# Attention scores per head: one matmul over an interleaved q transpose, or two over 64 partitions each

## The chip, the cores and the metric

The kernel runs as one program on one core of a Trainium2 chip. The metric is the device time of one execution in microseconds (us). A profiled execution has its own time and its own span, the stretch from its first to its last instruction in the trace. Engines are named as in the profile: PE is the matrix engine (PEld its weight loads), DVE the vector engine, ACT the scalar engine, POOL the general engine, SP the engine whose queue issues most DMA transfers.

## The reference, cut to what matters

Three layers run one after the other: local attention, a dense layer with a rational activation, and a gated sum over eight experts. Only the attention is touched.

```python
batch, n_heads, seq, head_dim = (4, 8, 576, 64)
scores = scale * np.matmul(q, k.transpose(0, 1, 3, 2))
rel = pos[:, None] - pos[None, :]
mask_plain = (rel >= 0) & (rel < 32)                      # heads 0 to 3
mask_dil = (rel >= 0) & (rel < 128) & (rel % 4 == 0)      # heads 4 to 7
scores = np.where(mask, scores, -1e9)
attn = softmax(scores)
x = attn @ v          # (2304, 512) after the heads are put side by side
h = x @ w_in;  g = P(h) / Q(h);  y = g @ w_out
out = sum over e of gate[:, e] * (relu(y @ w1[e]) @ w2[e])
```

## The kernel before, in words

**Three stages.** The attention of batch 0 runs first, in the order that `att_pieces(0)` lists. Then come 96 steps of the dense layer (`rat_l1`, `rat_a`, `rat_b`, `rat_c`, `rat_l2`), and the attention of batches 1, 2 and 3 is spread over the slots between them: `ATT` gives batch 1 to steps 0 to 7, batch 2 to steps 7 to 23 and batch 3 to steps 40 to 62. Last come the experts (`moe_l1`, `moe_l2`), in which no attention is left.

**One pair of heads.** Heads are taken in pairs, 16 pairs in all (4 batches of 4). The 64 dimensions of the two heads lie one above the other on 128 partitions. `att_prep` transposes q and k of a pair on PE, half a sequence at a time: three or four transposes (L352) into one PSUM bank, then copies into SBUF. k's transpose `kT` is copied as it is, by ACT (L362). q's transpose `qT` is kept in a blown-up form of shape 128 x 576 x 2: column (s, 0) holds head 0 of position s on partitions 0 to 63 and zeros below, column (s, 1) zeros above and head 1 on partitions 64 to 127. So q's bank is copied twice, the upper half by ACT (L366), the lower half by DVE (L364), each with a stride of two elements; the zeros are set once per tile at the start (L329), since there are two such tiles in all, one for even and one for odd pairs of batches 0 and 1.

**One group of scores.** `att_qk` handles 192 positions of a pair: three blocks of 64 positions, whose scores against 96 keys lie side by side in one PSUM bank, 128 rows (position, head) by 288 columns. First a 16-bit matmul with the identity adds the mask (L374, 128 rows by 288 columns). Then one matmul in 32-bit floats per block (L380) takes 128 columns of the blown-up `qT` as weights and 96 columns of `kT` as the moving operand. The trace shows each such matmul as two weight loads and two passes, so a group has six. There are 48 groups. The softmax follows on DVE (L398), ACT (L400), DVE (L404, L405) and POOL (L406). `att_tr` transposes the probabilities (L415, copied by ACT at L420), and `att_av` multiplies by v with six matmuls of 96 rows by 64 columns (L439, twelve passes), three for each half of the columns of PE; its moving operand is read with a stride of two.

**Order.** PE, DVE, ACT and POOL each work in the order in which they are given instructions. The pieces are laid into slots by hand, and the order of instructions is then fixed by a planner that simulates a timeline (`schedule_with_timeline_sim=True`). SP issues the loads in its own order; loads made by `load()` (L159) also wait for the latest mask matmul of batch 0 or the first matmul of a step (`gate_mm`, L376 and `rat_l1`).

Of the kernel before, what the change touches and what calls it, by code (L numbers as in the profile page):

```python
# [28 lines left out]
def kernel(  # L29
# [14 lines left out]
    nc = tc.nc  # L44
    B, H, S, D = q.shape
# [4 lines left out]
    P = 128  # L50
# [8 lines left out]
    KW = 96  # L59
# [173 lines left out]
    ident = cpool.tile([P, P], F32, name="ident")  # L233
    make_identity(nc, ident)
    nc.vector.memset(one, 1.0)
    ident_b = cpool.tile([P, P], BF16, name="ident_b")
    nc.vector.tensor_copy(ident_b, ident)
    SEAMS = (0, None, None, None, 32, None, 0, None, 16, 48, -16, None)
    masks = cpool.tile([P, 12, KW], BF16, name="masks")
    nc.gpsimd.memset(masks[:, 0], 0.0)  # L240
    nc.gpsimd.affine_select(out=masks[:, 0], in_=masks[:, 0], pattern=[[2, KW]], compare_op=ALU.is_ge, fill=NEG, base=-1, channel_multiplier=-1)
    nc.gpsimd.affine_select(out=masks[:, 0], in_=masks[:, 0], pattern=[[-2, KW]], compare_op=ALU.is_ge, fill=NEG, base=64, channel_multiplier=1)
    nc.vector.tensor_copy(masks[:, 1:12], masks[:, 0:1].to_broadcast([P, 11, KW]))
    for i, x in enumerate(SEAMS):
        if x is None:
            continue
        m = masks[:, i, 0:32 + x]
        if x <= 0:
            nc.gpsimd.memset(m, NEG)
        else:  # L250
            nc.gpsimd.affine_select(out=m, in_=m, pattern=[[0, 32 + x]], compare_op=ALU.is_ge, fill=NEG, base=2 * x - 1, channel_multiplier=-1)
    MASK_AT = {(0, 0): 0, (0, 1): 1, (0, 2): 1, (1, 0): 6, (1, 1): 3, (1, 2): 9}

    abt = cpool.tile([P, 8], F32, name="abt")
# [66 lines left out]

    def att_qk_tiles(alt):
        if alt:
            t = room("W3", [P, 3 * S + 32], F32)
            qT, kT = t[:, 0:2 * S].rearrange("p (s h) -> p s h", h=2), t[:, 2 * S:]
        else:
            qT = room("aqT", [P, S, 2], F32)
            kT = room("akT", [P, S + 32], F32)
        nc.vector.memset(qT, 0.0)  # L329
        nc.vector.memset(kT[:, 0:32], 0.0)  # L330
        return qT, kT

    def att_prep(b, pr, x):
        st = att[b, pr]
        which, y = divmod(x, 2)
        key = "ak" if which else "aq"
        src = st[key]
# [5 lines left out]
        if which == 0:  # L343
            outs = tuple((h * D, (h + 1) * D, st["qT"][:, :, h]) for h in range(2))
        else:
            outs = ((0, P, st["kT"][:, 32:]),)
        if y == 1:
            st.pop(key)
        w, n = (QB, 3) if pr < 2 else (72, 4)
        bt = bank("qkps")  # L350
        for c in range(n):
            nc.tensor.transpose(bt[:, c * w:(c + 1) * w], src[:, n * y + c, :, :].rearrange("p h d -> p (h d)"), ident[:w, :w])  # L352

        def after():
            for p0, p1, d in outs:
                if pr < 2:
                    dv, ps = d[p0:p1, y * HS:(y + 1) * HS], bt[p0:p1, 0:HS]
                else:
                    dv = d[p0:p1, :].rearrange("m (c w) -> m c w", c=4)[:, :, y * 72:(y + 1) * 72]
                    ps = bt[p0:p1, 0:HS].rearrange("m (c p) -> m c p", c=4)  # L360
                if which:
                    nc.scalar.activation(dv, ps, AF.Copy)  # L362
                elif p0 == D:
                    nc.vector.tensor_scalar(out=dv, in0=ps, scalar1=QSCALE, scalar2=None, op0=ALU.mult)  # L364
                else:
                    nc.scalar.activation(dv, ps, AF.Copy, scale=QSCALE)  # L366

        return after

    def att_qk(b, pr, jj):  # L370
# [6 lines left out]
        qf = st["qT"].rearrange("p s h -> p (s h)")  # L377
        for i in range(3):
            j = 3 * jj + i
            nc.tensor.matmul(  # L380
                bt[:, i * KW:(i + 1) * KW],
                qf[:, j * P:(j + 1) * P],
                st["kT"][:, j * 64:j * 64 + KW],
                start=False,
                stop=i == 2,
            )
        sc = bt[:, 0:3 * KW].rearrange("q (i c) -> q i c", i=3)
        i = b * NG + pr * 3 + jj
        sx = sb.tile([P, 4, 3], F32, tag="asx", bufs=4, name="sx")
# [41 lines left out]

    def att_av(b, pr, jj):
        st = att[b, pr]
        pT = st.pop(("pT", jj)).rearrange("k (i q h) -> k i q h", i=3, h=2)
        vt = att.pop(("v", b * NG + pr * 3 + jj))
        bt = bank("avps")
        for h in range(2):
            for i in range(3):
                nc.tensor.matmul(  # L439
                    bt[h * D:(h + 1) * D, i * 64:(i + 1) * 64],  # L440
                    vt[:, i, h, :],
                    pT[:, i, :, h],
                    start=True,
                    stop=True,
                )
# [899 lines left out]
```

## Time and profile before

| | us |
|---|---|
| three runs | 2025.17, 2027.48, 2030.88; median 2027.48 |
| the profiled execution, its own time | 2025.65 |
| its span in the trace | 2023.9 |
| PE busy | 1896.6 (94% of the span) |
| DVE busy | 1625.1 (80%) |
| ACT busy | 1235.8 (61%) |

The shares are averages over stages with different limits, so they have to be read again stage by stage: attention of batch 0 alone until the first step of the dense layer at 66.1 us, steps with the attention of batches 1 and 2 until about 268 us, steps without attention, steps with the attention of batch 3 from about 336 to 478 us, steps without attention, and the experts from 633 us to the end. A row of a window lists the busy time of each engine, the number of instructions in brackets, the granted clock of PE (1.00 is 2.4 GHz, 0.50 is 1.2 GHz), the share of the DMA engines and what they moved. Matmuls are pipelined: the distance from one start to the next says more than the duration of one.

### The profile page before, as it was taken

To read this page: it belongs to the slowest core of one execution; us is meant where nothing else is said; L and a number is where in the kernel's file an instruction comes from. 1 tells how busy PE (TensorE), PEld (TensorE's weight loads), DVE (VectorE), ACT (ScalarE), POOL (GpSimd) and SP (SyncE) were. 2 spreads that over 40 slices of the span, in tenths; PEclk is the share of its full clock that TensorE was granted. 3 is DMA by queue.
4 is the path that set the end of the run, shared out by engine and by line. 5 is a ranking of instruction groups with operands and counts; after the bars stand their busy time and mean duration, and the time that the engine had idled before them with its cause. 6 is when DMAs were issued, how large, how long until landed. Compare 5 with 4: busy or idle time off the path is not lost. (4 is left out here: it accounts for less than half of the span.)

```text
span 2023.9 us, 36375 instructions
## 1 busy us (share of the span) xinstructions
PE 1896.6 (94%) x13914; PEld 1428.6 (71%) x13914; DVE 1625.1 (80%) x2784; ACT 1235.8 (61%) x2328; POOL 486.8 (24%) x490
## 2 busy tenths in 40 slices
PE   7688899998989789999999999999999999999997
PEld 6466667876766566777777777777777777777776
DVE  5898899899998878778877877878778787787754
ACT  5777777776776536565654655556566466565543
POOL 1232233222222003112411511421231241141111
PEclk7688999999999899999999999999999999999999
DMA  6642220124310333146346345435534634543323
GB/s 174 167 142 77 60 75 14 33 65 143 105 41 12 120 105 110 62 127 160 72 109 170 67 104 144 110 62 135 154 64 107 175 78 105 152 87 79 87 55 47
DMA packets 209791, 200.06 MB, mean 99 GB/s; under 512 B 78288, under 2 KB 160208, under 8 KB 209616
## 3 DMA queue, kind: packets, MB, share of 16 engines
q1 hardware_dynamic: 192480, 164.70, 26.9%
q0 software_dynamic: 17136, 33.03, 10.9%
q8 instruction: 109, 1.79, 0.4%
q14 instruction: 66, 0.54, 0.1%
HBM read 151.67 MB, written 46.01 MB: 98 GB/s over the span
## 5 line engine op out<-in xcount | busy, mean ns | idle before, releaser
L925 PEld LDWEIGHTS <-roomA 128*128 128x128 f16 x3276 | 321.9, 99 | 197.6 <-issue 32.2
L925 PE MATMUL l1a<-roomA 128*128 128x384 f16 x1872 | 358.8, 328 | 4.8 <-ACT roomV L974 3.7
L925 PE MATMUL l1b<-roomA 128*128 128x384 f16 x1404 | 277.3, 329 | 14.1 <-DVE roomA L976 6.7
L683 POOL TENSOR_TENSOR roomIG<-roomA,roomIG 128x384 fp32r<-128x384 f32 x96 | 112.2, 1169 | 289.2 <-ACT roomIG L682 214.8
L947 POOL TENSOR_TENSOR roomIG<-roomA 128x384 f32<-128x384 f32 x48 | 60.7, 1264 | 464.4 <-ACT roomA L981 314.1
L1016 PE MATMUL yps<-roomA,roomV 128*128 128x256 f16 x630 | 170.3, 274 | 2.0 <-DVE roomV L1039 1.3
L1016 PE MATMUL yps<-roomA 128*128 128x256 f16 x630 | 169.6, 273 | 2.5 <-DVE roomV L1040 1.5
L1017 PE MATMUL yps<-roomA,roomV 128*128 128x256 f16 x630 | 171.5, 274 | 0.0
L1017 PE MATMUL yps<-roomA 128*128 128x256 f16 x630 | 170.8, 273 | 0.0
L1018 PE MATMUL yps<-roomA,roomV 128*128 128x256 f16 x630 | 170.6, 274 | 0.0
L1018 PE MATMUL yps<-roomA 128*128 128x256 f16 x630 | 169.4, 273 | 1.0 <-DVE roomA L992 1.0
L645 PE MATMUL h1ps<-roomA 128*128 128x384 f16 x384 | 131.5, 343 | 15.4 <-DVE roomA L665 7.9
L698 PE MATMUL o1ps<-roomIG,roomV 128*128 128x384 f32 x384 | 137.1, 357 | 4.3 <-POOL roomIG L683 4.1
L874 POOL TENSOR_TENSOR roomA<-roomA 128x256 f32<-128x256 f32 x140 | 130.1, 948 | 37.3 <-DVE roomA L888 23.6
L646 PE MATMUL h1ps<-roomA 128*128 128x384 f16 x384 | 130.7, 340 | 0.0
L699 PE MATMUL o1ps<-roomIG,roomV 128*128 128x384 f32 x384 | 130.6, 340 | 0.0
L888 DVE SCALAR_TENSOR_TENSOR roomA<-roomA,sm 128x768 f16<-128x768 f32 (+1 forms) x92 | 113.7, 1249 | 21.1 <-ACT roomA L885 19.8
L647 PE MATMUL h1ps<-roomA 128*128 128x384 f16 x384 | 130.4, 339 | 0.0
L947 POOL TENSOR_TENSOR roomIG<-roomV 128x384 f32<-128x384 f32 x48 | 50.0, 1041 | 323.5 <-ACT roomV L981 304.7
L697 PE MATMUL o1ps<-roomIG,roomV 128*128 128x384 f32 x384 | 106.1, 377 | 15.9 <-ACT roomIG L682 14.2
L1016 PEld LDWEIGHTS <-roomA 128*128 128x128 f16 x1008 | 98.6, 98 | 30.6 <-DVE roomA L1040 3.7
L1017 PEld LDWEIGHTS <-roomV 128*128 128x128 f16 x1008 | 99.0, 98 | 25.0 <-issue 1.5
(221 smaller groups left out, 5081.6 us busy)
## 6 DMA issues: line engine op xcount, KB each, us to landing
roomA<-xd SPq DMA_DIRECT2D x119, 384.0 KB
roomA<-in_moe_w_dram SPq DMA_DIRECT2D x256, 128.0 KB
roomA<-in_moe_w_dram SPq DMA_DIRECT2D x128, 256.0 KB
out_dram<-roomV POOLq DMA_DIRECT2D x32, 512.0 KB, 6.0
out_dram<-roomA POOLq DMA_DIRECT2D x31, 512.0 KB, 6.1
roomV<-in_moe_w_in_dram SPq DMA_DIRECT2D x16, 512.0 KB
roomA<-in_moe_w_out_dram SPq DMA_DIRECT2D x16, 512.0 KB
xd<-roomA SPq DMA_DIRECT2D x14, 384.0 KB
```

Of the source, the lines that this page charges most:

```text
L645: mm = nc.tensor.matmul(hp, whi, xb[:, 0, kk, :], start=kk == 0, stop=False)
L646: nc.tensor.matmul(hp, whi, xb[:, 1, kk, :], start=False, stop=False)
L647: nc.tensor.matmul(hp, wlo, xb[:, 0, kk, :], start=False, stop=kk == KD - 1)
L683: nc.gpsimd.tensor_tensor(out=gl, in0=g, in1=gh.bitcast(F32), op=ALU.subtract)
L698: nc.tensor.matmul(ob[dd], hi, d["gl"], start=False, stop=False)
L699: nc.tensor.matmul(ob[dd], lo, d["gh"], start=False, stop=last)
L874: pin("p" if pool else "v", eng.tensor_tensor(out=d[:, o, :], in0=a, in1=b, op=ALU.add if w == 0 and n == 0 else ALU.subtract))
L888: pin("v", nc.vector.scalar_tensor_tensor(out=l, in0=x, scalar=sc, in1=h, op0=ALU.mult, op1=ALU.subtract))
L925: mm = nc.tensor.matmul(ps, w[:, wx_, wh, kk * P:(kk + 1) * P], x[:, xh, kk, :], start=start and kk == 0 and wh == 0 and xh == 0, stop=sto ...
L1016: nc.tensor.matmul(o, hh[:, a - 1, c], w[:, m, 0, :], start=i == 0 and half == 0, stop=False)
L1017: nc.tensor.matmul(o, hh[:, a - 1, c], w[:, m, 1, :], start=False, stop=False)
L1018: nc.tensor.matmul(o, hl[:, a - 1, c], w[:, m, 0, :], start=False, stop=i == NP - 1 and (half == 1 or b == 3))
```

## The change

`qT` is kept in the form of `kT`, 128 x 576, and its bank is copied by one ACT instruction on 128 partitions, with the scale; the copy on DVE and the two clearings of `qT` go. Each block's scores are made by two matmuls, one for each head, over 64 partitions: head 0 from partitions 0 to 63 to PSUM rows 0 to 63, head 1 from partitions 64 to 127 to PSUM rows 64 to 127. The rows of a group are now (head, position), so the moving operand of `att_av` is read without a stride. The masks and the identity that adds them need 64 partitions; the identity is two 64 x 64 identities side by side.

```diff
-    ident_b = cpool.tile([P, P], BF16, name="ident_b")
-    nc.vector.tensor_copy(ident_b, ident)
+    ident_b = cpool.tile([D, P], BF16, name="ident_b")
+    nc.vector.tensor_copy(ident_b.rearrange("p (h c) -> p h c", h=2), ident[0:D, 0:D].unsqueeze(1).to_broadcast([D, 2, D]))
...
-    masks = cpool.tile([P, 12, KW], BF16, name="masks")
+    masks = cpool.tile([D, 12, KW], BF16, name="masks")
...
-            qT = room("aqT", [P, S, 2], F32)
+            qT = room("aqT", [P, S], F32)
...
-        nc.vector.memset(qT, 0.0)
...
-            for p0, p1, d in outs:
...
-                if which:
-                    nc.scalar.activation(dv, ps, AF.Copy)
-                elif p0 == D:
-                    nc.vector.tensor_scalar(out=dv, in0=ps, scalar1=QSCALE, scalar2=None, op0=ALU.mult)
-                else:
-                    nc.scalar.activation(dv, ps, AF.Copy, scale=QSCALE)
+            nc.scalar.activation(dv, ps, AF.Copy, scale=1.0 if which else QSCALE)
...
-            nc.tensor.matmul(
-                bt[:, i * KW:(i + 1) * KW],
-                qf[:, j * P:(j + 1) * P],
-                st["kT"][:, j * 64:j * 64 + KW],
-                start=False,
-                stop=i == 2,
-            )
+            for h in range(2):
+                hd = slice(h * D, (h + 1) * D)
+                nc.tensor.matmul(
+                    bt[hd, i * KW:(i + 1) * KW],
+                    st["qT"][hd, j * 64:(j + 1) * 64],
+                    st["kT"][hd, j * 64:j * 64 + KW],
+                    start=False,
+                    stop=i == 2,
+                )
...
-        pT = st.pop(("pT", jj)).rearrange("k (i q h) -> k i q h", i=3, h=2)
+        pT = st.pop(("pT", jj)).rearrange("k (i h q) -> k i h q", i=3, h=2)
...
-                    pT[:, i, :, h],
+                    pT[:, i, h, :],
```

## Rows read from the trace of the kernel before

**Rows 1.** Page, busy time, share of span and instructions of each engine.

```profile
PE 1896.6 (94%) x13914; PEld 1428.6 (71%) x13914; DVE 1625.1 (80%) x2784; ACT 1235.8 (61%) x2328; POOL 486.8 (24%) x490
```

**Rows 2.** Busy time by stage: length, PE, PEld, DVE, ACT, POOL, clock, DMA.

```profile
0.00:66.00 66.00, 42.75 (x326) 36.87 (x326) 39.35 (x129) 38.49 (x146) 12.25 (x33) 0.73 0.65 180
66.00:160.00 94.00, 73.86 (x519) 56.97 (x520) 84.89 (x186) 71.36 (x217) 29.06 (x31) 0.86 0.48 141
160.00:268.00 108.00, 94.01 (x668) 72.74 (x667) 90.20 (x218) 83.47 (x242) 27.10 (x32) 0.94 0.26 69
...
336.00:478.00 142.00, 135.09 (x983) 107.22 (x981) 129.64 (x257) 104.77 (x281) 37.70 (x40) 0.98 0.24 67
...
633.00:2023.90 1390.90, 1350.25 (x10250) 1005.22 (x10248) 1061.20 (x1616) 775.52 (x1127) 316.34 (x304) 0.99 0.42 104
```

**Rows 3.** Single lines: durations in ns (min/median/max), first and last start, shapes.

```profile
L364 DVE TENSOR_SCALAR roomA<-qkps x24: 455/461/464, 5.5 to 429.5; 64x288 f32<-64x288 f32 x24
...
L366 ACT ACTIVATE roomA<-qkps x24: 409/426/502, 5.0 to 428.5; 64x288 f32<-64x288 f32 x24
...
L362 ACT ACTIVATE roomA<-qkps x24: 390/411/430, 6.2 to 433.0; 128x288 f32<-128x288 f32 x24
...
L329 DVE MEMSET roomA<- x1: 1018/1018/1018, 1.1 to 1.1; 128x1152 f32 x1
```

**Rows 4.** Busy time of line 364 alone in four stages: length, DVE.

```profile
0.00:66.00 66.00, 3.69 (x8) 0.73 0.65 180
66.00:160.00 94.00, 4.45 (x10) 0.86 0.48 141
160.00:268.00 108.00, 2.68 (x6) 0.94 0.26 69
336.00:478.00 142.00, 3.61 (x8) 0.98 0.24 67
```

**Rows 5.** DMA issues of SP, 38 to 64 us: start, length, line, count.

```profile
40.10 3.79 SPq L316 DMA_DIRECT2D roomA<-in_v_dram  x5
44.84 1.64 SPq L274 DMA_DIRECT2D roomA<-in_q_dram  x2
47.79 0.86 SPq L274 DMA_DIRECT2D roomA<-in_k_dram  x2
48.75 7.24 SPq L316 DMA_DIRECT2D roomA<-in_v_dram  x13
```

**Rows 6.** Timeline of PE, 448.4 to 450.8 us: start, length, line, count.

```profile
448.48 0.29 PE L374 MATMUL scps<-masks,ident_b 128*128 128x288 bf16 x1
448.61 0.80 PE L380 MATMUL scps<-roomA 128*128 128x96 f32 x6
449.19 0.42 PE L697 MATMUL o1ps<-roomIG,roomV 128*128 128x384 f32 x1
449.45 0.34 PE L698 MATMUL o1ps<-roomIG,roomV 128*128 128x384 f32 x1
449.63 0.34 PE L699 MATMUL o1ps<-roomIG,roomV 128*128 128x384 f32 x1
449.90 0.74 PE L439 MATMUL avps<-roomA 96*64 96x64 f32 x12
450.57 0.34 PE L645 MATMUL h1ps<-roomA 128*128 128x384 f16 x1
```

**Rows 7.** Timeline of PE, 468.0 to 469.1 us, two groups of L439 together.

```profile
468.02 1.09 PE L439 MATMUL avps<-roomA 96*64 96x64 f32 x24
469.04 0.44 PE L699 MATMUL o1ps<-roomIG,roomV 128*128 128x384 f32 x1
```

**Rows 8.** PE in two slices of 0.1 us, inside L380, inside L439.

```profile
448.80:448.90 0.10, 0.10 (x3) 1.00 0.00 0
450.30:450.40 0.10, 0.10 (x8) 1.00 0.00 0
```

**Rows 9.** Longest wait of PE, 66 to 268 us: total, times, longest.

```profile
PE scps L374 <- ACT roomV L362: 5.2, 1, 5.2
```

More of the change, by code (lines that the diff above doesn't have):

```diff
@@ L235 @@
     nc.vector.memset(one, 1.0)
-    ident_b = cpool.tile([P, P], BF16, name="ident_b")
-    nc.vector.tensor_copy(ident_b, ident)
+    ident_b = cpool.tile([D, P], BF16, name="ident_b")
+    nc.vector.tensor_copy(ident_b.rearrange("p (h c) -> p h c", h=2), ident[0:D, 0:D].unsqueeze(1).to_broadcast([D, 2, D]))
     SEAMS = (0, None, None, None, 32, None, 0, None, 16, 48, -16, None)
-    masks = cpool.tile([P, 12, KW], BF16, name="masks")
+    masks = cpool.tile([D, 12, KW], BF16, name="masks")
     nc.gpsimd.memset(masks[:, 0], 0.0)
-    nc.gpsimd.affine_select(out=masks[:, 0], in_=masks[:, 0], pattern=[[2, KW]], compare_op=ALU.is_ge, fill=NEG, base=-1, channel_multiplier=-1)
-    nc.gpsimd.affine_select(out=masks[:, 0], in_=masks[:, 0], pattern=[[-2, KW]], compare_op=ALU.is_ge, fill=NEG, base=64, channel_multiplier=1)
-    nc.vector.tensor_copy(masks[:, 1:12], masks[:, 0:1].to_broadcast([P, 11, KW]))
+    nc.gpsimd.affine_select(out=masks[:, 0], in_=masks[:, 0], pattern=[[1, KW]], compare_op=ALU.is_ge, fill=NEG, base=-1, channel_multiplier=-1)
+    nc.gpsimd.affine_select(out=masks[:, 0], in_=masks[:, 0], pattern=[[-1, KW]], compare_op=ALU.is_ge, fill=NEG, base=32, channel_multiplier=1)
+    nc.vector.tensor_copy(masks[:, 1:12], masks[:, 0:1].to_broadcast([D, 11, KW]))
     for i, x in enumerate(SEAMS):
@@ L250 @@
         else:
-            nc.gpsimd.affine_select(out=m, in_=m, pattern=[[0, 32 + x]], compare_op=ALU.is_ge, fill=NEG, base=2 * x - 1, channel_multiplier=-1)
+            nc.gpsimd.affine_select(out=m, in_=m, pattern=[[0, 32 + x]], compare_op=ALU.is_ge, fill=NEG, base=x - 1, channel_multiplier=-1)
     MASK_AT = {(0, 0): 0, (0, 1): 1, (0, 2): 1, (1, 0): 6, (1, 1): 3, (1, 2): 9}
@@ L323, in att_qk_tiles @@
         if alt:
-            t = room("W3", [P, 3 * S + 32], F32)
-            qT, kT = t[:, 0:2 * S].rearrange("p (s h) -> p s h", h=2), t[:, 2 * S:]
+            t = room("W3", [P, 2 * S + 32], F32)
+            qT, kT = t[:, 0:S], t[:, S:]
         else:
-            qT = room("aqT", [P, S, 2], F32)
+            qT = room("aqT", [P, S], F32)
             kT = room("akT", [P, S + 32], F32)
-        nc.vector.memset(qT, 0.0)
         nc.vector.memset(kT[:, 0:32], 0.0)
@@ L342, in att_prep @@
             st["qT"], st["kT"] = att["qkT", alt]
-        if which == 0:
-            outs = tuple((h * D, (h + 1) * D, st["qT"][:, :, h]) for h in range(2))
-        else:
-            outs = ((0, P, st["kT"][:, 32:]),)
+        d = st["kT"][:, 32:] if which else st["qT"]
         if y == 1:
@@ L354, in after @@
         def after():
-            for p0, p1, d in outs:
[L356 to L360, printed above, removed]
-                if which:
-                    nc.scalar.activation(dv, ps, AF.Copy)
-                elif p0 == D:
-                    nc.vector.tensor_scalar(out=dv, in0=ps, scalar1=QSCALE, scalar2=None, op0=ALU.mult)
-                else:
-                    nc.scalar.activation(dv, ps, AF.Copy, scale=QSCALE)
+            if pr < 2:
+                dv, ps = d[:, y * HS:(y + 1) * HS], bt[:, 0:HS]
+            else:
+                dv = d.rearrange("m (c w) -> m c w", c=4)[:, :, y * 72:(y + 1) * 72]
+                ps = bt[:, 0:HS].rearrange("m (c p) -> m c p", c=4)
+            nc.scalar.activation(dv, ps, AF.Copy, scale=1.0 if which else QSCALE)
         return after
@@ L376, in att_qk @@
             gate_mm[0] = mm.ins
-        qf = st["qT"].rearrange("p s h -> p (s h)")
         for i in range(3):
             j = 3 * jj + i
-            nc.tensor.matmul(
-                bt[:, i * KW:(i + 1) * KW],
-                qf[:, j * P:(j + 1) * P],
-                st["kT"][:, j * 64:j * 64 + KW],
-                start=False,
-                stop=i == 2,
-            )
+            for h in range(2):
[7 more added lines that the diff above has]
+                )
         sc = bt[:, 0:3 * KW].rearrange("q (i c) -> q i c", i=3)
```

## The prediction

> **What bounds the kernel now.** I first read the page's busy times [rows 1]: PE is busy 94% of the span, DVE 80%. That average does not say what a change in the attention is worth, so the next view is the table by stage [rows 2]. The experts' stage, 1391 of 2024 us, has PE busy 97% and holds nothing of the attention. It will only start earlier or later. What can change lies before 633 us, in four stretches with different limits.
>
> In the first 66 us no engine is near full (PE 43, DVE 39, ACT 38 of 66). The SP queue is: it issues transfers one behind the other [rows 5], and between 40.10 and 56.0 us it stands still only from 43.89 to 44.84 and from 46.48 to 47.79, 2.3 us in all. The dense layer's weights (L159) are issued in this same queue. Faster attention can recover at most such gaps.
>
> From 66 to 160 us DVE is busy 84.9 of 94 us (90%), PE 73.9, ACT 71.4: DVE is the limit, with batch 1's attention on top of the conversion of weights. From 160 to 268 us DVE has 84% and PE 87%, from 336 to 478 us DVE 91% and PE 95%: there the two alternate, and neither is worth its full time.
>
> **The copies of q.** A copy on DVE takes 0.46 us [rows 3]; there are 32, of which 8, 10, 6 and 8 lie in the four stretches [rows 4]. All go. Nothing takes their place on DVE. ACT still makes one copy per bank; on 128 partitions and without a stride such a copy takes 0.41 us (L362) against 0.43 us (L366), 32 times 0.02 us, which I count as nothing in either direction, because ACT has idle time in every stretch.
>
> - 66 to 160 us: 10 x 0.46 = 4.6 us. At DVE's 90% I take 4.1 us. Ends: 2.3 and 4.6.
> - 160 to 268 us: 6 x 0.46 = 2.8 us. PE is as busy, so I take half, 1.4 us. Ends: 0 and 2.8.
> - 336 to 478 us: 8 x 0.46 = 3.7 us. PE is busier, so I take a third, 1.2 us. Ends: 0 and 3.7.
> - Before 66 us: 8 copies, and two clearings of 1.02 us each (L329). Behind the clearings stand the casts of the masks, which the first scores need, but these wait for q's transfer and ACT's copies anyway. Ends: 0 and the 2.3 us in which SP stands still; I take 0.7 us, near the lower end, since SP is what fills this stretch.
>
> Together 7.4 us off. No transfer is added or moved. Those paced by the mask matmul are released with it, at most as much earlier as the attention gets. The q tile's second half is ready earlier by one DVE copy; the score matmuls then wait for ACT's copy alone. No wait is added. What is late next at the head of the attention is ACT's copy of k: PE's longest wait from 66 to 268 us is for it, 5.2 us [rows 9], and this change leaves it where it is. The masks' instructions keep their free sizes, so POOL's part costs the same.
>
> **The scores on PE.** Six passes per group become twelve. In a stretch at full clock the mask matmul starts at 448.48, the score passes at 448.61, the next work at 449.19 [rows 6]: 0.71 us per group. The six passes last 0.80 us, the end of the last one included (about 0.28 us): (0.80 - 0.28) / 5 = 0.105 us per pass of 128 weight columns.
>
> What twelve passes of 64 weight columns cost is not shown for scores, but `att_av` has twelve such passes in two halves of PE's columns. One group of it takes 449.90 to 450.57, 0.67 us; two groups back to back take 468.02 to 469.04, 1.02 us [rows 6, 7]. So twelve more passes add 0.35 us, 0.029 us per pass, and 0.32 us belong to getting in and out. Halving the columns alone would explain 0.053 us. The rest is the two halves working beside each other: a slice inside L439 touches eight matmuls, one inside L380 three [rows 8]. Entering the half-width form costs a little as well: L699 to L439 is 0.27 us, L698 to L699 0.18 us, so 0.09 us, say 0.1.
>
> After the change a group is: enter the 64-row form for the mask (0 or 0.1), mask 0.13, enter the 64 by 64 form (0 or 0.1), twelve passes with both heads beside each other, 0.35 us with no cost at the ends and 0.67 us with `att_av`'s. That gives 0.48 us at the lower and 1.00 us at the upper end, against 0.71: from 0.23 us less to 0.29 us more. I take 0.81, 0.10 us more. It lies nearer to the row of `att_av`, because the loads are the same size; it lies below it, because the heads alternate in the queue and need not start one behind the other. In the DVE-bound stretch this is hidden by DVE. It counts in the 24 groups of batches 2 and 3, by the share that PE has there: 12 x 0.10 x 1/2 + 12 x 0.10 x 2/3 = 1.4 us more. Ends: 24 x 0.23 = 5.5 us less, 24 x 0.29 = 7.0 us more.
>
> In batch 0 PE is not the limit, and I count nothing there, with the same SP gaps as bound. The moving operand of `att_av` loses its stride; nothing in the trace shows that the stride costs anything, I take zero, and at best it could halve the 0.029 us of 24 x 12 passes, 4.2 us less.
>
> **The sum** is 7.4 - 1.4 = 6.0 us off the profiled execution's 2025.65 us: 2019.7 us. The median of the runs is 2027.48 us, 1.8 us higher; from it the forecast is 2021.5 us. With all terms at their good ends except the stride, 11.1 + 2.3 + 5.5 = 18.9 us less, 2009; with DVE's gain at 2.3 us and PE's cost at 7.0 us, 2032. Less than 0.3%, 6 us here, can hardly be told from no change, so the forecast sits right at that edge.
>
> **Rivals.**
>
> *The heads run one behind the other, and PE pays for it (slower).* Both heads write the same PSUM bank, from different halves of PE's rows. Nothing in the trace shows two such matmuls at once; `att_av` uses only different halves of the columns. If they exclude each other, the twelve passes cost 12 x 0.053 = 0.64 us in place of 0.35, and a group 0.10 + 0.13 + 0.64 + 0.32 = 1.19 us, 0.48 us more than now. The place where that decides is the 24 groups between 160 and 478 us: 11.5 us more. DVE's saving there is then lost behind PE; the 4.1 and 0.7 us before remain, and about 2.3 us of batch 1's extra PE time show: 11.5 + 2.3 - 4.8 = 9 us more, 2036 us. It gets slower by over 6 us from (6 + 4.8) / 24 = 0.45 us more per group on. For it: no row with different halves of rows. Against it: with different halves of columns the overlap is complete. The Trainium skill, TensorEngine Tiling (Array Packing), section Restrictions and Gotchas, says that different row tiles cannot access the same PSUM bank simultaneously; by that rule this rival would be the outcome, and no run here shows it so far.
>
> *More than forecast.* PE changes its form at no cost, both heads overlap, and DVE's saving shows nearly whole: 11 to 19 us less, 2009 to 2016, say 2012 us. For it: DVE's copies stand in its queue ahead of the steps' own work. Against it: the price of entering at L439.
>
> *The saving is hidden.* PE, and waits such as ACT's copy of k, set the pace in all stretches; the first one returns half of 4.1 us, and PE's 1.4 us takes most of it: about 2026.5 us, no change. For it: 95% of PE from 336 us on. Against it: 90% of DVE before 160 us.
>
> *Another order.* The planner sees twelve passes where it saw six, and may lay pieces differently. A displaced piece can make or remove a wait like the one of 5.2 us [rows 9]. It has no direction; I widen the forecast's own range by it.
>
> That the change does not do what it says can be left out: one copy in the place of two stands in the code, line by line.
>
> **How the numbers follow.** Forecast (2 to 11 us less, 2016 to 2026): 0.55, of which 0.31 lie beyond 6 us and 0.24 within it. More than forecast: 0.15, all faster. Hidden: 0.12, all within. Slower, 2034 and above: 0.18. So faster 0.46, same 0.36, slower 0.18. The range for 8 in 10 runs from 2010 to 2036: it takes in the lower bound but for the last 2 us, the upper bound of 2032, and the slower rival up to its computed time, leaving about 0.07 below and 0.1 above.
>
> **What will show it.** Right if: L364 is gone from DVE's list and DVE's busy time falls by about 16.8 us (32 copies and two clearings); ACT's copies of q take 0.41 us; the first step of the dense layer starts at 65 to 66 us; the work that reached to 160 us ends 4 to 5 us earlier; a group at full clock takes 0.7 to 0.9 us from mask to next work; the experts start at 627 us in place of 633. Wrong if: twelve score passes take over 1 us (the heads exclude each other); the score passes show idle PE ahead of them at each change of form; DVE's idle time between 66 and 160 us grows by as much as was removed (the saving hidden); or the experts' stage itself changes its length, for which nothing in the change gives a reason.

## The result and the profile after

| | before | after |
|---|---|---|
| median of the runs, us | 2027.51 (four runs) | 2008.91 (four runs, 2006.81 to 2012.47) |
| the profiled execution, its own time | 2025.65 | 2012.47 |
| its span | 2023.9 | 2010.7 |

The ratio is 0.9909, with an interval of 0.9889 to 0.9929: 18.6 us less, where 6.0 were forecast; the time lies 1 us below the range. The profiled execution is the longest of the four runs after; its span is 13.2 us shorter than before, so the trace shows about two thirds of the gain.

The page's busy times of the changed kernel, engine by engine:

```profile
PE 1901.3 (95%) x14202; PEld 1421.6 (71%) x14202; DVE 1598.4 (79%) x2750; ACT 1237.7 (62%) x2328; POOL 484.0 (24%) x490
```

Beside [rows 1], DVE has 34 instructions fewer, the 32 copies and the two clearings, and PE has 288 matmuls more, six in each of the 48 groups. DVE's busy time fell by 26.7 us, where the prediction's sign was 16.8; the experiments show where the rest comes from.

Two rows of the table by stage of the changed kernel, with the same bounds and columns as [rows 2]:

```profile
66.00:160.00 94.00, 78.48 (x601) 57.20 (x602) 79.19 (x184) 73.58 (x227) 29.38 (x32) 0.81 0.46 137
...
336.00:478.00 142.00, 138.79 (x1074) 106.96 (x1073) 129.72 (x255) 107.75 (x285) 39.26 (x40) 0.99 0.26 75
```

Between 66 and 160 us DVE is now busy 79.2 us instead of 84.9. Its idle time grew by 5.7 us, and the stretch did not get shorter, as the next table shows.

**Where the time went.** Every step of the dense layer begins with the same matmuls (h1ps, L645 before, L636 after, 384 in 96 steps), and the experts with the same 289 matmuls of their first layer (L925 before, L916 after). Counted in the order of time, these give marks at which two traces can be compared. Times in us from the start of the span of each profile; the kernels in the last four columns are experiments, described below.

| mark | before | after | new work, old order | old work, new order | new scores, two copies, new order | new dense, old experts |
|---|---|---|---|---|---|---|
| step 0 | 66.1 | 67.3 | 66.0 | 66.7 | 67.0 | 66.3 |
| step 8 | 159.2 | 160.3 | 158.6 | 161.6 | 165.1 | 159.3 |
| step 24 | 268.5 | 268.6 | 267.6 | 272.0 | 275.6 | 267.7 |
| step 40 | 335.8 | 332.4 | 334.9 | 335.6 | 339.2 | 332.0 |
| step 64 | 478.0 | 469.2 | 479.9 | 472.9 | 477.6 | 467.7 |
| first expert matmul | 633.1 | 627.4 | 635.2 | 631.9 | 635.9 | 626.7 |
| 289th expert matmul | 740.8 | 727.4 | 741.8 | 731.6 | 736.5 | 731.8 |
| end | 2023.9 | 2010.7 | 2025.0 | 2015.4 | 2018.6 | 2013.7 |

The marks are not exact. Four of the kernels below have the same work in the same order up to step 8, and their traces reach it at 158.6, 159.3, 159.6 and 161.4 us; so a difference of up to 3 us between two marks can be chance.

From before to after, nothing is gained up to step 24 (268.5 and 268.6). Then 3.5 us come off in steps 24 to 40, where there is no attention at all, 5.4 in steps 40 to 64, and 3.1 are given back until the first expert. From there to the 289th matmul 7.7 us come off, 107.7 against 100.0; the remaining 1283 us are equal within 0.2. Steps 24 to 40 do not hold quite the same instructions in both (PE 363 and 354 matmuls), so the sum up to the first expert is the safer figure: 5.7 us.

The experts' opening in one row, up to the 289th matmul of the first layer, columns as in [rows 2]. First the kernel before, then after.

```profile
633.10:740.85 107.75, 95.83 (x681) 68.28 (x679) 87.14 (x168) 51.57 (x83) 13.34 (x11) 0.92 0.21 69
```

```profile
627.30:727.45 100.15, 90.32 (x677) 65.07 (x675) 83.22 (x166) 51.27 (x81) 11.21 (x11) 1.00 0.24 75
```

Of the 7.6 us, 2.1 are idle time of PE (11.9 against 9.8), and 5.5 us are busy time. The kernel before has only four matmuls more in its row: nearly the same matmuls ran longer. The granted clock, 1.00 after, was 0.92 before. PE's waits there, in the kernel before (us in total, times, longest):

```profile
PE l1b L925 <- DVE roomA L976: 6.7, 1, 6.7
PE lgps L768 <- DVE roomV L225: 2.6, 3, 1.2
```

and in the changed kernel:

```profile
PE l1a L916 <- ACT roomA L965: 3.4, 3, 2.5
PE lgps L759 <- DVE roomV L225: 0.7, 1, 0.7
```

Around the long wait of the kernel before, PE alone (length, PE busy, clock, DMA share, GB/s):

```profile
686.60:693.30 6.70, 0.03 (x2) 0.70 0.09 27
693.30:700.00 6.70, 6.70 (x32) 0.54 0.18 52
```

and two groups of twelve matmuls of one form in its timeline, the first behind the three waits of L768, which end between 667 and 671 us (start, length, line, count):

```profile
670.65 4.00 PE L925 MATMUL l1a<-roomA 128*128 128x384 f16 x12
...
676.33 2.11 PE L925 MATMUL l1b<-roomA 128*128 128x384 f16 x12
```

Behind the 6.7 us in which PE stood still, the clock was 0.54, nearly the lower of its two levels (1.2 of 2.4 GHz), for the next 6.7 us; and behind the three shorter waits, between which PE had only matmuls of 8 and 16 columns, twelve matmuls took 4.00 us where the same number took 2.11 a little later. So these waits cost their own length and some microseconds at a lower clock behind them. In the changed kernel no wait of this stretch is longer than 2.5 us, and the clock stayed at 1.00. No instruction of the stretch was edited. The order of the work differs; the experiments below show that it decides.

**The edit's own instructions.** The copies did what was forecast, the scores on PE cost more. The copy lines of q and k together (durations min, median, max in ns):

```profile
L356 ACT ACTIVATE roomA<-qkps x48: 389/413/543, 4.9 to 424.5; 128x288 f32<-128x288 f32 x48
```

Scores back to back on PE at full clock, in the changed kernel (start, length, line, count):

```profile
162.13 0.33 PE L638 MATMUL h1ps<-roomA 128*128 128x384 f16 x1
162.39 0.29 PE L364 MATMUL scps<-masks,ident_b 64*128 64x288 bf16 x1
162.61 0.71 PE L371 MATMUL scps<-roomA 64*64 64x96 f32 x12
163.26 0.29 PE L364 MATMUL scps<-masks,ident_b 64*128 64x288 bf16 x1
...
164.13 0.29 PE L364 MATMUL scps<-masks,ident_b 64*128 64x288 bf16 x1
164.35 0.71 PE L371 MATMUL scps<-roomA 64*64 64x96 f32 x12
164.99 0.44 PE L689 MATMUL o1ps<-roomIG,roomV 128*128 128x384 f32 x1
```

and the same place in the kernel before:

```profile
161.04 0.33 PE L647 MATMUL h1ps<-roomA 128*128 128x384 f16 x1
161.20 0.29 PE L374 MATMUL scps<-masks,ident_b 128*128 128x288 bf16 x1
161.32 0.80 PE L380 MATMUL scps<-roomA 128*128 128x96 f32 x6
161.97 0.29 PE L374 MATMUL scps<-masks,ident_b 128*128 128x288 bf16 x1
```

From mask to mask a group takes 0.87 us after and 0.77 before; from the work ahead to the first mask 0.26 and 0.16. The time from mask to scores grew from 0.12 to 0.22, so each of these two changes of form costs 0.10 us, and the twelve passes take no longer than the six. In front of work over 128 rows the difference is larger: from mask to next work 0.86 us after (164.13 to 164.99) and 0.71 before [rows 6]. The starts of the single passes in the traces show why: from the first to the last there are 0.47 us after and 0.53 before, but from the last one to the next work 0.17 after and 0.06 before, so leaving the 64 by 64 form costs 0.11 us as well. With 0.10 us for the entry ahead of the mask, such a group costs 0.25 us more than before. The two heads do run beside each other, as a slice of 0.1 us inside L371 shows (length, PE with the number of matmuls touched, clock, DMA share, GB/s):

```profile
162.85:162.95 0.10, 0.10 (x8) 1.00 0.02 3
```

Eight matmuls, as many as in the slice inside L439 of [rows 8].

### The profile page after: what moved, and what is told of

It is laid out like the page before. It is cut to its first block, busy times and chain, and to the rows that moved or that the text cites. A ratio compares the mean times of both kernels' runs of the same rounds, so it can differ in the third digit from the quotient of the medians.

```text
span 2010.7 us, 36918 instructions
## 1 busy us (share of the span) xinstructions
PE 1901.3 (95%) x14202; PEld 1421.6 (71%) x14202; DVE 1598.4 (79%) x2750; ACT 1237.7 (62%) x2328; POOL 484.0 (24%) x490
## 5 line engine op out<-in xcount | busy, mean ns | idle before, releaser
L916 PEld LDWEIGHTS <-roomA 128*128 128x128 f16 x3276 | 320.7, 98 | 196.3 <-issue 29.2
L916 PE MATMUL l1a<-roomA 128*128 128x384 f16 x1872 | 356.4, 327 | 8.8 <-ACT roomV L965 3.9
L916 PE MATMUL l1b<-roomA 128*128 128x384 f16 x1404 | 276.0, 328 | 10.1 <-DVE gs L191 4.1
L689 PE MATMUL o1ps<-roomIG,roomV 128*128 128x384 f32 x384 | 140.2, 365 | 6.7 <-POOL roomIG L674 6.4
L636 PE MATMUL h1ps<-roomA 128*128 128x384 f16 x384 | 129.4, 337 | 11.4 <-ACT roomA L411 4.2
L690 PE MATMUL o1ps<-roomIG,roomV 128*128 128x384 f32 x384 | 132.8, 346 | 0.0
L637 PE MATMUL h1ps<-roomA 128*128 128x384 f16 x384 | 129.2, 336 | 0.0
L638 PE MATMUL h1ps<-roomA 128*128 128x384 f16 x384 | 128.9, 336 | 0.0
L1008 PEld LDWEIGHTS <-roomV 128*128 128x128 f16 x1008 | 98.6, 98 | 24.8 <-issue 1.7
L1007 PEld LDWEIGHTS <-roomV 128*128 128x128 f16 x1008 | 98.8, 98 | 24.2 <-DVE roomV L1030 1.6
```

What stands on the lines that cost most here:

```text
L636: mm = nc.tensor.matmul(hp, whi, xb[:, 0, kk, :], start=kk == 0, stop=False)
L637: nc.tensor.matmul(hp, whi, xb[:, 1, kk, :], start=False, stop=False)
L638: nc.tensor.matmul(hp, wlo, xb[:, 0, kk, :], start=False, stop=kk == KD - 1)
L689: nc.tensor.matmul(ob[dd], hi, d["gl"], start=False, stop=False)
L690: nc.tensor.matmul(ob[dd], lo, d["gh"], start=False, stop=last)
L916: mm = nc.tensor.matmul(ps, w[:, wx_, wh, kk * P:(kk + 1) * P], x[:, xh, kk, :], start=start and kk == 0 and wh == 0 and xh == 0, stop=sto ...
```

## The experiments

The traces suggest that the order made the difference, and an order can be forced. Twelve kernels were run in three groups of four, each group on one chip, with the kernel before beside it; a kernel was executed 4 to 11 times. The theories named in the expectations are that the gain is the work removed, or that it is the new order which the planner laid because the work had changed. Each verdict is the ratio of the kernel's time to that of the kernel before, with its 95% interval.

An order is forced at the end of the program. Every engine's instructions are listed as they were made, put in the order of a stored permutation, and each is made to follow the one before it, with no semaphore:

```diff
+    for e, text in _ORDER.items():
+        steps = _np.frombuffer(zlib.decompress(base64.b85decode(text)), dtype="<i2")
+        places = _np.cumsum(steps.astype(_np.int64)).tolist()
+        seq = [made[e][p] for p in places]
+        for a, b in zip(seq, seq[1:]):
+            tc.add_manual_dep(b, a.name, mybir.DependencyInfo(mybir.DependencyClass.NoSync, mybir.DependencyReason.SCHED_ONLY))
```

Below "old order" is that of the kernel before on all engines and "new order" that of the changed kernel; where an instruction exists in one only (the copies on DVE, the clearings), it keeps the place that the planner gives it. The diffs of these kernels say in words which permutation stands in `_ORDER`; the code is the same.

### Work and order exchanged

**The new work in the old order.** The changed kernel, with every engine held to the order of the kernel before.

```diff
-PE, DVE, ACT, POOL, SP: the changed kernel's order
+PE, DVE, ACT, POOL, SP: the order of the kernel before
```

> The changed kernel's instructions, but every engine is given them in the order of the kernel before (the two removed kinds left out, each score matmul replaced in place by its two). Theory A (the work that was removed makes the gain): about the time of the changed kernel, 2009 us, at most 4 us above it, and the opening of the experts' stage shortened as there. Theory B (the planner's new order makes most of it, above all the 7 us at the opening of the experts' stage): 2016 to 2024 us, with the gain gone behind 633 us. Theory C (the removed work gives 6 us as forecast, the order the rest): 2020 to 2023 us.

Measured: 2025.41 us, ratio 0.9990 (0.9981 to 0.9999). Of the 18.6 us, 2.5 are left (2027.9 - 2025.4); all three theories had expected a lower time, B up to 2024 us. Its row from 66 to 160 us, columns as in [rows 2]:

```profile
66.00:160.00 94.00, 77.46 (x595) 56.60 (x596) 79.29 (x177) 71.12 (x216) 28.98 (x31) 0.83 0.49 142
```

DVE has lost 5.6 us of work beside [rows 2], and the mark of step 8 moved by 0.6 us. What DVE waited for there, in the kernel before:

```profile
DVE roomA L663 <- ACT roomA L662: 2.7, 2, 1.7
DVE roomA L506 <- ACT roomA L502: 2.2, 1, 2.2
DVE roomA L225 <- ACT roomA L222: 1.4, 3, 0.5
```

and in this run, whose line numbers behind the edit are nine lower (L506 is L497 here, L663 is L654):

```profile
DVE roomA L497 <- ACT roomA L493: 4.3, 2, 3.3
DVE roomA L654 <- ACT roomA L653: 3.6, 2, 2.2
DVE roomA L225 <- ACT roomA L222: 2.2, 3, 1.3
```

The three waits for ACT, 6.3 us in sum, became 10.1 us, which is 3.8 of the 5.6 us: DVE has less to do and waits at the same instructions for ACT. The opening of the experts is nearly as long as before, same view as above:

```profile
635.10:741.85 106.75, 94.15 (x681) 67.36 (x680) 87.18 (x168) 51.53 (x83) 13.36 (x11) 0.95 0.21 70
```

So the removed work alone does not carry the gain.

**The old work in the new order.** The kernel before, held to the order of the changed kernel; the 32 copies on DVE and the clearings stay in.

```diff
-PE, DVE, ACT, POOL, SP: the order of the kernel before
+PE, DVE, ACT, POOL, SP: the changed kernel's order
```

> The instructions of the kernel before, in the order of the changed kernel; the DVE copies of q and the two clearings are left to the planner to place. Theory A: 2025 to 2028 us, as before, or slower. Theory B: 2011 to 2017 us, with the experts' stage opening as fast as in the changed kernel. Theory C: 2013 to 2017 us.

Measured: 2019.38 us, ratio 0.9957 (0.9940 to 0.9974). Without any of the edit, the order alone takes 8.5 us off (2027.9 - 2019.4), between what A expected and the 2011 to 2017 us of B and C. The opening of the experts has the new length, same view:

```profile
631.80:731.65 99.85, 91.78 (x677) 65.86 (x675) 82.27 (x165) 50.54 (x80) 11.04 (x10) 0.98 0.23 75
```

Steps 24 to 40, without attention, are a second sign. Before, in this stretch:

```profile
268.50:335.80 67.30, 62.73 (x363) 46.47 (x361) 65.17 (x109) 51.46 (x108) 26.82 (x21) 1.00 0.12 41
```

the new work in the old order:

```profile
267.60:334.90 67.30, 62.73 (x362) 46.48 (x359) 65.17 (x109) 51.30 (x108) 26.75 (x21) 1.00 0.14 41
```

and the old work in the new order:

```profile
272.00:335.60 63.60, 61.03 (x353) 44.73 (x352) 60.45 (x101) 49.57 (x105) 24.41 (x19) 1.00 0.12 42
```

The first two agree to 0.01 us on PE and DVE; the length goes with the order, and 63.8 us is what the changed kernel has. But 8.5 and 2.5 us make 11.0, not 18.6: the two parts are worth more together than apart.

The order also decides how long DVE's instructions take. The pages of these two runs, the new work in the old order first:

```profile
PE 1906.2 (94%) x14202; PEld 1422.2 (70%) x14202; DVE 1610.5 (80%) x2750; ACT 1236.4 (61%) x2328; POOL 487.9 (24%) x490
PE 1895.7 (94%) x13914; PEld 1431.7 (71%) x13914; DVE 1611.2 (80%) x2784; ACT 1239.0 (61%) x2328; POOL 484.7 (24%) x490
```

Against 1625.1 us before, the removed work takes 14.6 us off DVE, and the new order takes 13.9 us off without removing one instruction. The largest part of the latter lies in the 96 instructions of L675 (L666 in the changed kernel): 71.8 us before, 71.6 with the new work in the old order, 63.7 with the old work in the new order, 64.1 after. Before, 66 of them ran with no instruction of POOL beside them and took 0.61 us on average, the other 30 took 1.05 us; in the new order fewer of them meet POOL (22 and 24), and for a shorter time. How much of the gain in time this carries was not tried apart.

### The copies and the scores apart

In the next kernels the scores are the changed ones, but q's copy is again shared by ACT and DVE, 64 partitions each, without a stride and without the clearings.

```diff
-            nc.scalar.activation(dv, ps, AF.Copy, scale=1.0 if which else QSCALE)
+            if which:
+                nc.scalar.activation(dv, ps, AF.Copy)
+            else:
+                nc.scalar.activation(dv[0:D], ps[0:D], AF.Copy, scale=QSCALE)
+                nc.vector.tensor_scalar(out=dv[D:P], in0=ps[D:P], scalar1=QSCALE, scalar2=None, op0=ALU.mult)
```

**In the old order**, with `_ORDER` of the kernel before:

> The changed kernel, but q's bank is copied half by ACT and half by DVE, as before, only without the stride; order of the kernel before on every engine. Against the kernel before only the score matmuls differ (and the two clearings). If PE's extra 0.10 to 0.25 us per group counts: 0 to 5 us slower than before, 2027 to 2032 us. If the DVE copies are what matters, it lies above the same order without them by 6 to 9 us. If the copies are hidden, by less than 3 us.

Measured: 2026.88 us, ratio 1.0001 (0.9986 to 1.0016). With the order of before and its copies, the new scores change nothing that can be measured. The copies themselves are then worth 1.5 us (2026.9 - 2025.4; by the ratios 2.2), less than the intervals can tell from nothing, and the two traces reach the first expert matmul at 635.0 and 635.2 us.

**In the planner's own order**, with no order forced:

> The changed kernel with the copy of q split between ACT and DVE again, order left to the planner. Theory A: the gain goes back by 8 to 16 us, to 2017 to 2025 us. Theory B: any time from 2005 to 2030 us, since the planner lays a third order, and the time follows that order and not the 14.7 us of DVE copies. Theory C: 6 to 8 us above the changed kernel plus whatever the new order brings.

Measured: 2028.68 us, ratio 1.0001 (0.9990 to 1.0012). For this work the planner lays a third order, which is not the new one: its first expert matmul comes at 647.0 us. So this run does not tell what the copies cost in the new order.

**In the new order**, with `_ORDER` of the changed kernel, the copies on DVE where the planner puts them:

> The changed kernel's order on every engine, but q's bank copied half by ACT and half by DVE, the DVE copies placed by the planner. If the DVE copies are worth something only in this order (they explain the 10 us between old and new work in the new order): 2014 to 2019 us. If the score matmuls or the clearings explain that difference: 2008 to 2011 us.

Measured: 2020.36 us, ratio 0.9962 (0.9948 to 0.9976). Against the changed kernel's 2008.9 us the copies cost 11.5 us in the new order (by the ratios 10.7: 0.9962 - 0.9909, times 2027.5), a little more than was expected if they count in this order, though they are the same instructions as in the old one:

```profile
L360 DVE TENSOR_SCALAR roomA<-qkps x24: 453/460/461, 5.4 to 429.9; 64x288 f32<-64x288 f32 x24
L360 DVE TENSOR_SCALAR roomV<-qkps x8: 453/460/461, 18.0 to 134.2; 64x288 f32<-64x288 f32 x8
```

32 x 0.46 = 14.7 us of DVE's time. They also last as long as the strided ones of [rows 3]. The loss in the trace arises early: 4.8 us by step 8, 7.0 by step 24, then 6.8, 8.4, 8.5 at the later marks and 7.9 at the end. PE waits for such a copy (L360) twice between 66 and 165 us, 0.4 us and:

```profile
PE scps L375 <- DVE roomV L360: 1.3, 1, 1.3
```

and DVE waits there for scores in turn:

```profile
DVE sx L393 <- PE scps L375: 4.7, 2, 4.1
```

where the changed kernel has, between 66 and 160 us:

```profile
DVE sx L389 <- PE scps L371: 2.3, 1, 2.3
```

These waits name some of the loss; how the rest is passed on through the queues this run does not take apart. The old work in the new order has its copies on DVE too, and its trace is only 1.3 us behind the changed kernel's at step 8, 3.4 at step 24 and 4.5 at the first expert matmul; so the place of the loss is not certain.

The four kernels with the new scores, in us:

| | q copied by ACT and DVE | q copied by ACT alone |
|---|---|---|
| old order | 2026.9 | 2025.4 |
| new order | 2020.4 | 2008.9 |

The order is worth 6.5 us with the copies and 16.5 without (by the ratios 7.9 and 16.4). The old scores with the clearings give 2027.5 in the old and 2019.4 in the new order, within about 1 us of the first column: the change on PE does not show in either order. The intervals leave room for 3 us either way in the old order and 4.5 in the new.

### Which part of the order

**The old order up to the first expert matmul, the new one behind it**, with the new work:

```diff
-PE, DVE, ACT, POOL, SP: new order throughout
+PE, DVE, ACT, POOL, SP: old order up to the first matmul of L916, new order behind it
```

> The changed kernel's instructions; up to the first expert matmul every engine has the order of the kernel before, from there on the order of the changed kernel. Theory B1 (the opening of the experts' stage is a separate piece of luck in the order, worth 7 to 8 us wherever it starts): 2017 to 2019 us, with first expert matmul to the 289th in about 100 us in place of 107. Theory B2 (the opening is fast only because the new order reaches it with less work left over): about 2025 us, with about 107 us.

Measured: 2021.68 us, ratio 0.9969 (0.9957 to 0.9981). The opening of the experts took 100.4 us in its trace: the new length follows the order of the experts' own part, as B1 has it; the time lies between the two theories.

**The reverse, new before the experts, old behind it**, with the new work:

```diff
-PE, DVE, ACT, POOL, SP: new order throughout
+PE, DVE, ACT, POOL, SP: new order up to the first matmul of L916, old order behind it
```

> The reverse: the order of the changed kernel up to the first expert matmul, the order of the kernel before from there on. Theory B1: 2015 to 2018 us, first to 289th expert matmul in about 107 us. Theory B2: about 2009 to 2011 us, about 100 us.

Measured: 2015.01 us, ratio 0.9929 (0.9917 to 0.9941). The opening took 105.2 us; length and time are as B1 expected. From the old order throughout (2025.4), the dense stage's new order is worth 10.4 us and the experts' 3.7; both together are worth 16.5. By the ratios, which compare each kernel with the kernel before on its own chip, it is 12.4, 4.3 and 16.4 us: within the noise these two parts add up.

**The old order to step 8, the new one from there**, with the new work:

```diff
-PE, DVE, ACT, POOL, SP: new order throughout
+PE, DVE, ACT, POOL, SP: old order up to step 8 (about 159 us), new order behind it
```

> The changed kernel's instructions; the order of the kernel before up to the ninth step of the dense layer (about 159 us), where it was ahead by 2 us in the profiles, then the order of the changed kernel. If the parts of an order add up: 2005 to 2008 us, 2 us faster than the changed kernel. If the later order only recovers what the start left: 2009 us, no difference.

Measured: 2011.32 us, ratio 0.9914 (0.9900 to 0.9927). That is 2 us above what either theory had, but by the ratio (0.9909 for the changed kernel) not to be told from it. The order before step 8 is worth little: what counts stands behind it.

**The old order, but steps 8 to 12 in the new one**, with the new work. In these steps the traces differ most for their length, 32.1 us before and 27.0 after. PE's waits in them, before:

```profile
PE mxps L173 <- ACT p L400: 3.3, 1, 3.3
PE mxps L173 <- DVE roomA L665: 1.8, 1, 1.8
PE ptps L415 <- DVE sm L187: 1.2, 1, 1.2
```

and the longest after:

```profile
PE scps L371 <- ACT roomA L356: 1.2, 1, 1.2
```

```diff
-PE, DVE, ACT, POOL, SP: new order throughout
+PE, DVE, ACT, POOL, SP: old order, with steps 8 to 12 in the new order
```

> The changed kernel's instructions in the order of the kernel before, except for steps 8 to 12 of the dense layer (159 to 187 us), which have the order of the changed kernel: there the old order held PE for 6.3 us around one small matmul (L173). If the places add up: 4 to 5 us under the same work in the old order throughout, 2020 to 2022 us. If the time is lost again later: 2024 to 2026 us.

Measured: 2025.35 us, ratio 0.9988 (0.9978 to 0.9998), as the old order throughout. In its trace steps 8 to 12 took 25.9 us (161.4 to 187.3), so step 12 came 3.4 us earlier than in the old order throughout (190.7); but step 24 came at 270.6 us, against 267.6 there. The gain of one place was lost again within twelve steps. (Up to step 8 the order is that of the old order throughout, which got there at 158.6 us: by the lengths of the stretches, some 6 us were gained in steps 8 to 12 and some 6 lost from 12 to 24.) PE's longest waits from step 12 to 24 in this run:

```profile
PE scps L364 <- DVE roomA L225: 2.7, 1, 2.7
PE h1ps L636 <- DVE roomA L656: 1.8, 1, 1.8
```

The first of them does not stand among the waits of the old order throughout there, whose longest is the second one, 1.8 us.

**A third order for the new work**, the one that the planner laid for the two copies:

```diff
-PE, DVE, ACT, POOL, SP: new order throughout
+PE, DVE, ACT, POOL, SP: the planner's order of the kernel with two copies
```

> The changed kernel's instructions in the order that the planner made for the variant with two copies (its DVE copies of q left out). Theory B (time follows the order): 2022 to 2029 us, within 6 us of that variant's 2028.7, with the first expert matmul at 640 us or later. Theory A (time follows the removed work): 2009 to 2015 us.

Measured: 2024.57 us, ratio 0.9981 (0.9970 to 0.9992). Its opening of the experts is short (99.2 us), but the first expert matmul comes at 642.8 us. The same work has now taken 2025.4, 2024.6 and 2008.9 us in three whole orders, and 2011 to 2025 us in mixtures of two: the planner's order for the changed kernel is the good one among those run, and its orders for nearly the same work need not be.

### Single waits

**The wait at the experts' opening, in the kernel before.** PE waits 6.7 us for L976 at 686.6 us. Twelve neighbouring instructions of DVE were permuted, so that those on which PE waits (L947, L976) come ahead of work for later (weights, L874 and L888, and gates, L787 to L789).

```diff
-DVE: L787 L874 L874 L888 L947 L788 L874 L947 L789 L874 L976 L947
+DVE: L947 L947 L976 L947 L787 L874 L874 L888 L788 L874 L789 L874
```

> The kernel before, work and order, but for twelve neighbouring DVE instructions near 690 us: the three additions of L947 and the eviction of L976, for which PE waited 6.67 us, go ahead of the preparation of the next weights (L874, L888) and of the gate's iteration (L787 to L789). If that one place in the order carries a lasting part of the 4 to 6 us at the experts' opening: PE's wait falls to 2 to 4 us and the time to 2023.5 to 2025.5 us. If PE only meets the same delay at the next wait, because the weights come later: 2027 to 2029 us, no change.

Measured: 2029.08 us, ratio 1.0001 (0.9992 to 1.0010): no gain. PE's waits between 640 and 760 us in this run:

```profile
PE l1b L925 <- DVE roomA L976: 4.4, 1, 4.4
PE l1b L925 <- DVE gs L191: 3.7, 2, 3.4
PE smps L173 <- DVE gs L792: 1.7, 1, 1.7
```

The first wait became 2.3 us shorter. The second is not new: it lies further on, at 755 us in the kernel before:

```profile
PE l1b L925 <- DVE gs L191: 3.6, 2, 3.3
```

New are the third, at 697 us, and one of 0.5 us for L979; together 2.2 us, they took back what was gained. The opening took 107.5 us at a clock of 0.94. With its order forced and twelve instructions moved, the kernel took no longer than before, so the forcing in itself costs nothing that shows.

**One instruction of the changed kernel moved.** There PE waits 3.9 us at 738 us, because DVE stands 3.5 us at L841 for a transfer of weights, ahead of the gate that PE needs (L191). L841 was put two places later.

```diff
-DVE: L841 L191 L983
+DVE: L191 L983 L841
```

> The changed kernel, work and order, with one DVE instruction moved by two places: the reduction of new weights (L841) that waited 3.5 us for its transfer near 740 us now stands behind the gate's sum (L191) and a subtraction (L983), so that PE need not wait 3.9 us for the bank that the gate's sum holds. If the order is what counts: 2005 to 2007 us, 2 to 4 us faster than the changed kernel. If the next wait takes it up: 2008 to 2010 us.

Measured: 2008.79 us, ratio 0.9906 (0.9892 to 0.9920), the changed kernel's own time. Two of PE's longest waits between 620 and 760 us in this run:

```profile
PE l1a L916 <- ACT roomV L965: 3.5, 1, 3.5
PE l1b L916 <- DVE roomV L975: 2.5, 1, 2.5
```

and the same two in the changed kernel, with the wait for L191:

```profile
PE l1b L916 <- DVE gs L191: 4.1, 2, 3.9
PE l1a L916 <- ACT roomV L965: 3.0, 1, 3.0
PE l1b L916 <- DVE roomV L975: 0.7, 1, 0.7
```

For L191 PE now waits 0.5 us in place of 4.1, and most of the difference stands elsewhere: the listed waits of the stretch sum to 15.6 us against 16.8. This trace also shows how much executions differ: up to the 289th expert matmul its marks lie within 1.3 us of the changed kernel's, but the rest took 1279.3 us where the changed kernel's profile has 1283.3. No kernel run here is measurably faster than the changed one.

## Why the prediction was wrong, and where it was right

**Right: the copies; too low: the price of a group.** The copies and clearings are gone from DVE, and ACT's copy of q takes 0.41 us. A group of scores takes 0.86 us from mask to next work, within the 0.7 to 0.9 of the signs, but with the entry into the 64-row form, left open as 0 or 0.1 and measured as 0.10, it costs 0.25 us more than the 0.71 of before, where 0.10 was taken and 0.29 was the bad end. Back to back it is 0.10 (0.87 and 0.77). The forecast had its 0.35 us for twelve passes from L439, whose moving operand has 64 columns where the scores have 96; the passes took 0.47 from first to last start, and 0.17 to get out. In the time none of this shows: with copies on both engines the old and the new scores are within 1 us in either order, too close to tell the forecast's 1.4 us from nothing.

**Right: the heads overlap.** The slower rival fell: eight matmuls touch 0.1 us, and the passes of twelve last no longer than those of six. By the rule of the Trainium skill, TensorEngine Tiling (Array Packing), section Restrictions and Gotchas, two row tiles do not access one PSUM bank at the same time; in this trace matmuls of both heads, on different rows of PE and different partitions of one bank, run beside each other, and no time lost to that rule shows (0.47 us from the first to the last of twelve starts; 0.64 us was the price if they exclude each other).

**Wrong: the stretch to 160 us.** The forecast took 4.1 us off "at DVE's 90%", and the mark of step 8 moved from 159.2 to 160.3. Its own sign for this was named, that DVE's idle time grows by as much as was removed, and that is what happened: from 9.0 to 14.8 us between steps 0 and 8, the gaps summed (14.5 with the new work in the old order). In the old order this is the full answer, the rival "the saving is hidden": 2025.4 us measured, about 2026.5 forecast. A busy share of 90% did not make DVE the bound; ACT's results were late next, in three waits that grew from 6.3 to 10.1 us. The first 66 us gave nothing either: step 0 came at 66.0 us in the old order and at 67.3 in the changed kernel.

**Wrong, and the step that cost the forecast: the order as noise.** "Another order" was priced by one displaced wait of 5 us, "has no direction", and widened the range. Measured, the planner's new order is worth 6.5 us with the copies on DVE and 16.5 without, where the whole edit in the old order is worth 2.5. And the prediction held that the experts "will only start earlier or later". The planner orders the experts too, and the opening of that stage got 7.7 us shorter with the new order: 99.7 to 100.6 us in six kernels that have it there, 105.2 to 108.0 in six that have the old one. In the two profiles 5.5 us of this are longer busy time of PE at a lower clock; where only the order was exchanged, it is 3.8 of 6.6 us (new work) and 4.1 of 7.9 (old work), and the rest is idle time. The prediction knew the clock as 0.99 for the stage as a whole [rows 2] and did not look at it in the first 100 us.

**Near in size, in one order only, and by luck.** In the new order the copies cost 11.5 us, more than the 7.4 us that the forecast summed for them, and in the traces 7.9. By stretches of the table above, two copies less one in the new order, that is 5.1 us from step 0 to 8 (98.1 - 93.0; forecast 4.1), 2.2 to step 24 (110.5 - 108.3; 1.4) and 1.4 to step 64 (202.0 - 200.6; 1.2). The old work in the new order, with as many copies on DVE, gives 1.9, 2.1 and 0.3 us for the same stretches, and the marks can differ by 3 us by chance. So the prices by busy shares are of the right size in that order, no more, and several times too high in the old one. The experts start at 627.4 us, as the signs had it, and the prediction's sum of all good ends, 18.9 us, comes near the measured 18.6; both are luck, since the same work in the old order starts them at 635.2 us and takes 2.5 us off. "More than forecast", 2012 us at a chance of 0.15, was the rival nearest to the result; but its reason, that PE changes its form for nothing, is not what happened.

**What stays open.** Why the copies are hidden in one order and cost 11.5 us in the other was not settled. The loss begins before step 8 in the trace with the copies and the new scores, with DVE waiting for scores, and is smaller there with the old scores; whether it is the copies' duration or the places where the planner put them was not tried apart. Nor is it known which few instructions carry the order's gain: single waits and five steps did not.

## What to carry to other kernels

Where a planner fixes the order, an edit changes the work and the order at once: run the new work in the old order and the old work in the new one before the edit is given the credit. Forecast such a change with the order as a rival that has a size (here 6 to 16 us on 2027, with effects in stages that the edit does not touch), not as a margin. A share of busy time of 90% is no price per microsecond removed, and a single long wait that is removed may come back at the next instructions.

## What was not expected of the hardware

A wait of PE cost more than its length here: behind 6.7 us of standing still the clock was 0.54 for the next 6.7 us, and behind three waits of 2.6 us in sum twelve matmuls took 4.00 us in place of 2.11. Across the opening of the experts 681 matmuls took 95.8 us at a mean clock of 0.92, and 677 took 90.3 at 1.00.

Two matmuls on different halves of PE's rows, writing to different halves of the partitions of one PSUM bank, ran beside each other: twelve passes of 64 by 64 in 0.65 us from the first score start to the next mask (162.61 to 163.26), six of 128 by 128 in 0.65 us as well (161.32 to 161.97). Each change on the way in, from 128-row to 64-row and on to 64 by 64 forms, cost 0.10 us, start to start, and the way out to 128-row work 0.11.

Of 96 like instructions of DVE in the kernel before (L675), the 66 with POOL idle beside them took 0.61 us on average, the other 30 took 1.05.
